# Windowed attention, forward and backward, on one core: gradient loads held behind a transpose, a fourth y/z buffer, and whole 128x128 products in place of split ones

## The chip, the cores and the metric

The kernel runs on one core of one Trainium2 chip. The metric is the device time of the whole program in microseconds (us). Each figure is the median of several executions.

In this kernel TensorE multiplies matrices, VectorE (DVE) and ScalarE (ACT) copy its results out of its output memory, PSUM (they "evict" them), and do the softmax, POOL issues one queue of DMAs (gradient loads and output stores) and the sync engine (SP) issues the other (x loads and all DMA transposes). In the timelines below each engine works through its own instructions in the order in which the program gives them.

## The reference, cut to what matters

```python
# x, grad_out: (1, 256, 256, 384) bf16; windows of 8 x 8 = 64 tokens, C = 384 channels
qkv = xw @ wqkv                       # per window: 64 x 384
p = softmax(q @ k.T * C ** -0.5)
out = (p @ v) @ wo
# returned: out, and the gradients of x, wqkv and wo for grad_out
```

There are 1024 windows. The kernel takes eight at a time, a "quad" of four tiles of 128 tokens, so there are 128 steps. The weights are multiplied together once, at the start; the weight gradients are accumulated over the steps.

## The kernel before

The work on one quad is spread over four steps: loading and projecting (`a`), scores and softmax (`b`), the rest of the attention (`c`), and the gradient of x (`dx`, `d`). The names in what follows: `xq` and `dq` are x and the gradient of the output as loaded; `xT` and `dT` are their transposes, which `project` multiplies into `yz`; `tok` is the transpose of `yz`; `Uq` is a product of the attention and `UT` its transpose, which `dx` needs; `osb` and `dsb` are the buffers from which the output and the gradient of x are stored. `filler` is a piece of the weight gradients. What the change and the argument touch:

```python
def load(st):                                    # issued LEAD = 3 steps ahead
    st["xq"] = xq = grp.tile([P, QUAD, C], BF16, tag="xq", bufs=2 * GQ + 4)
    st["dq"] = dq = qp.tile([P, QUAD, C], BF16, tag="dq", bufs=6)
    for t in range(QUAD):
        nc.sync.dma_start(out=xq[:, t, :], in_=dram_tile(x, bp, t0 + t))
        nc.gpsimd.dma_start(out=dq[:, t, :], in_=dram_tile(grad_out, bp, t0 + t))

def to_channels(st, src, name):                  # dT <- dq, xT <- xq, UT <- Uq
    st[name] = dst = qp.tile([P, QUAD, CK, P], BF16, tag=name, bufs=3 if name == "xT" else 2)
    nc.sync.dma_start_transpose(out=..., in_=st[src]...)

def product(out, lhsT, rhs, start, stop):        # split: two column tiles of 128x64
    if split[0]:
        for h in (LO, HI):
            nc.tensor.matmul(out[h], lhsT=lhsT[:, h], rhs=rhs, start=start, stop=stop)
    else:
        nc.tensor.matmul(out, lhsT=lhsT, rhs=rhs, start=start, stop=stop)

# ... project: y/z evicted by ScalarE into st["yz"], bufs=3
# ... to_tokens: tok <- yz, a DMA transpose on nc.sync

def step(d, c, b, a):                            # the order of one step; cut
    B(scores) ... B(values) ... A(project) ... filler(1)
    pw = C_(attend, (2, 3)) ; B(turn)
    C_(to_channels, "Uq", "UT")
    C_(attend_end, (2, 3), pw)
    split[0] = True
    D_(dx, (0, 1)) ; filler(1)                   # needs tok and UT of the quad
    split[0] = False
    pw = B(attend, (0, 1)) ; B(attend_end, (0, 1), pw) ; D_(dx, (2, 3))

for i in range(-1, n + 2):
    to_channels(get(i + 2), "dq", "dT")
    to_channels(get(i + 2), "xq", "xT")
    load(get(i + LEAD))
    to_tokens(c)
    step(d, c, b, a)
```

So in every step the sync engine issues, in this order, `dT`, `xT`, four x loads, `tok`, `UT`. POOL issues four gradient loads and then the stores, each when its tile has been evicted.

## Time and profile before

| | before |
|---|---|
| time, median of 3 (lowest to highest) | 2145.0 us (2144.54 to 2149.26) |
| TensorE busy | 95% of the span |
| DMA engines busy, in every slice but the last | 90% or more |
| one step, mean over the span (score product to score product) | 16.3 us |
| one step in which TensorE never stalls | 14.8 us |

The two step times in the last rows are read from the timeline. The busy shares alone name two candidates for the bound. The Trainium skill ("Trainium Kernel Development and Optimization", "Performance Expectations") warns that matmul busy time is a bad metric for how close a kernel is to its roofline (the best that the chip allows), because matmuls are pipelined; this trace agrees: TensorE is "95% busy" although an average step is 1.5 us longer than it needs.

These lines are of the page of the kernel before: an engine with its busy time, share and instructions; the DMA engines' busy share in 40 slices; and the two DMA queues with packets, MB and the time of their packets as a share of 16 engines. q1 is the sync engine's queue, q0 POOL's.

```profile
PE 2021.4 (95%) x19046; PEld 1183.3 (55%) x19046; DVE 1280.2 (60%) x2851; ACT 1455.3 (68%) x3213; POOL 1122.7 (53%) x2054
...
DMA  9999999999999999999999999999999999999995
...
q1 hardware_dynamic: 1074384, 304.15, 85.6%
q0 software_dynamic: 98304, 151.39, 27.5%
```

Which of the two paces the step is told by who waits for whom. From the waits of the kernel before (engine and line, what it waited for; total us, times, longest us):

```profile
ACT yz L138 <- DMA tok<-yz: 328.0, 99, 7.2
...
PE po L242 <- ACT yz L138: 45.5, 72, 3.9
```

ScalarE is about to evict y/z and finds its buffer still being read by the `tok` transpose of an older quad. TensorE then waits for ScalarE. In the timeline (start us, length us, what, and in brackets the idle time before it) one such place looks like this:

```profile
1029.05 1.07 ACT L138 CAST yz<-pj 128x512 bf16<-128x512 f32 x2 [3.85 <-DMA tok<-yz]
...
1031.49 0.35 PE L242 MATMUL po<-uq,PS 64*64 64x384 bf16 x2 [0.85 <-ACT yz L138]
```

The transpose is late because the queue that issues it is. The sync engine's timeline shows no pause between its instructions, only about 0.1 to 0.2 us:

```profile
1008.25 1.47 SPq L116 DMA_TRANSPOSE UT<-Uq  x1
1009.94 3.12 SPq L116 DMA_TRANSPOSE dT<-dq  x1
1013.24 1.69 SPq L116 DMA_TRANSPOSE xT<-xq  x1
1014.98 2.89 SPq L111 DMA_DIRECT2D xq<-in_x_dram  x4
1017.98 6.78 SPq L144 DMA_TRANSPOSE tok<-yz  x1
1024.85 2.88 SPq L116 DMA_TRANSPOSE UT<-Uq  x1
1027.95 1.80 SPq L116 DMA_TRANSPOSE dT<-dq  x1
```

And that engine waits for hardly anything but the DMAs before its own.

```profile
SPq L116 <- DMA dq<-in_grad_out_dram: 1.3, 2, 0.9
```

(The larger entries of that view name compute instructions that were over long before; what they show is the time that the queue took to accept the transfer.) So the sync engine's queue, mostly transposes, paces the kernel: by this trace `UT` is issued 7.8 us (median) after its input is complete, and `dT` 9.0 us after its gradient has landed. The POOL queue, which has time to spare, issues its gradient loads right after the stores of the step, at 1011.57, 1.7 us before `xT` is issued:

```profile
1010.48 1.07 POOL L233 DMA_DIRECT2D out_dram<-dsb  x2 [2.44 <-DMA out_dram<-osb]
1011.57 2.11 POOL L112 DMA_DIRECT2D dq<-in_grad_out_dram  x4
1016.54 2.27 POOL L231 DMA_DIRECT2D out_dram<-osb  x4 [2.85 <-ACT osb L249]
```

The cost of splitting products is read from the chain of work that ended last (start us, length us, what and how many): 12 half products of `dx` against 6 whole ones, and 24 against 12 of the weight gradient.

```profile
2095.11 0.97 PE pd L124 x12
2096.08 1.95 PE pg L124 x24
...
2099.09 1.08 PE pd L126 x6
2100.17 1.95 PE pg L126 x12
```

### The profile page before, as it was taken

The numbers are of one execution on the slowest core, as the hardware profiler recorded it, in microseconds if no ns is written. First come the engines' busy times: TensorE is split into PE (matmuls) and PEld (weight loads), VectorE is DVE, ScalarE is ACT, GpSimd is POOL, SyncE is SP. The second block draws the span as 40 slices with busy tenths as digits, with TensorE's granted clock in tenths as the row PEclk, the third lists the DMA queues.
The fourth block names the chain that finished last, engine by engine and source line by source line (L and its number), as shares of the span: only waits on it lengthen the run. The fifth ranks groups of instructions, "written<-read, shape, count | busy, mean of one in ns | idle before, by whom it ended". The sixth has DMA issues, their size and how long they took to land. (4 is left out here: it accounts for less than half of the span.)

```text
span 2135.8 us, 51378 instructions
## 1 busy us (share of the span) xinstructions
PE 2021.4 (95%) x19046; PEld 1183.3 (55%) x19046; DVE 1280.2 (60%) x2851; ACT 1455.3 (68%) x3213; POOL 1122.7 (53%) x2054
## 2 busy tenths in 40 slices
PE   8899999999999999999999999999999999999998
PEld 4555555555555555555555555555555555555555
DVE  6565565656565656656565665665656565665664
ACT  6667676766676667767676766766666676666673
POOL 4554555555555545545454555554555455555543
PEclk9999999999999999999999999999999999999999
DMA  9999999999999999999999999999999999999995
GB/s 210 220 225 220 217 219 211 224 221 219 215 219 213 225 206 225 218 212 222 215 218 213 216 224 211 218 220 218 216 212 221 211 220 222 222 223 211 220 208 123
DMA packets 1173339, 459.11 MB, mean 215 GB/s; under 512 B 1056864, under 2 KB 1147744, under 8 KB 1173088
## 3 DMA queue, kind: packets, MB, share of 16 engines
q1 hardware_dynamic: 1074384, 304.15, 85.6%
q0 software_dynamic: 98304, 151.39, 27.5%
q8 instruction: 149, 2.44, 0.5%
q14 instruction: 102, 0.84, 0.1%
q10 hardware_dynamic: 400, 0.29, 0.0%
HBM read 101.84 MB, written 101.84 MB: 95 GB/s over the span
## 5 line engine op out<-in xcount | busy, mean ns | idle before, releaser
L231 POOL DMA_DIRECT2D out_dram<-osb x1024 | 578.3, 571 | 682.9 <-ACT osb L249 637.3
L138 ACT CAST yz<-pj 128x512 bf16<-128x512 f32 x384 | 213.4, 588 | 360.6 <-DMA tok<-yz 328.0
L286 DVE TENSOR_TENSOR GF_acc<-pg,GF_acc 128x384 f32<-128x384 f32 x258 | 143.9, 558 | 471.8 <-PE pg L124 269.0
L249 ACT CAST osb<-po 128x384 bf16<-128x384 f32 x512 | 225.1, 501 | 211.3 <-issue 174.8
L112 POOL DMA_DIRECT2D dq<-in_grad_out_dram x512 | 270.6, 537 | 174.2 <-DMA out_dram<-osb 63.8
L233 POOL DMA_DIRECT2D out_dram<-dsb x512 | 275.4, 541 | 136.4 <-DMA out_dram<-dsb 62.4
L250 DVE CAST Uq<-pu 128x384 bf16<-128x384 f32 x512 | 264.7, 550 | 54.9 <-PE pu L242 53.0
L126 PE MATMUL pv<-B_sb,xT 128*128 128x384 bf16 x1536 | 270.6, 326 | 0.0
L126 PE MATMUL pj<-xT,A_sb 128*128 128x512 bf16 x1152 | 269.5, 379 | 0.9 <-DMA xT<-xq 0.9
L126 PE MATMUL pj<-dT,BT_sb 128*128 128x512 bf16 x1152 | 269.5, 379 | 0.0
L224 ACT CAST uq<-pv 128x384 bf16<-128x384 f32 x512 | 242.7, 475 | 35.5 <-PE pv L126 33.3
L261 ACT CAST Wq<-pw 64x384 bf16<-64x384 f32 x512 | 242.5, 474 | 9.2
L273 ACT CAST dsb<-pd 128x384 bf16<-128x384 f32 x512 | 222.0, 482 | 26.0 <-ACT Wq L261 7.5
L124 PEld LDWEIGHTS <-xq 128*64 128x64 bf16 x3024 | 204.6, 111 | 45.6
L126 PEld LDWEIGHTS <-xq 128*128 128x128 bf16 x1560 | 152.6, 98 | 114.0
L140 ACT CAST yz<-pj 128x512 bf16<-128x512 f32 x384 | 201.3, 603 | 1.2 <-PE pj L126 1.1
L126 PEld LDWEIGHTS <-A_sb 128*128 128x128 bf16 x1152 | 112.6, 98 | 137.1 <-DMA xT<-xq 1.4
L242 PE MATMUL po<-uq,PS 64*64 64x384 bf16 x1024 | 145.0, 338 | 45.9 <-ACT yz L138 45.5
L126 PEld LDWEIGHTS <-xT 128*128 128x128 bf16 x1536 | 141.5, 98 | 82.8
L124 PE MATMUL pg<-Wq,xq 128*64 128x384 bf16 x2016 | 182.0, 329 | 0.0
L166 DVE TENSOR_REDUCE mx<-sd 64x4 f32<-64x256 f32 x256 | 108.1, 422 | 122.6 <-PE sd L153 118.6
L126 PE MATMUL pg<-Uq,xq 128*128 128x384 bf16 x1032 | 181.6, 326 | 0.0
(66 smaller groups left out, 2674.9 us busy)
## 6 DMA issues: line engine op xcount, KB each, us to landing
xq<-in_x_dram SPq DMA_DIRECT2D x512, 96.0 KB, 3.7
dq<-in_grad_out_dram POOLq DMA_DIRECT2D x512, 96.0 KB, 4.8
out_dram<-osb POOLq DMA_DIRECT2D x1024, 48.0 KB, 5.3
out_dram<-dsb POOLq DMA_DIRECT2D x512, 96.0 KB, 5.5
dT<-dq SPq DMA_TRANSPOSE x128, 6.5
xT<-xq SPq DMA_TRANSPOSE x128, 5.1
tok<-yz SPq DMA_TRANSPOSE x128, 10.2
UT<-Uq SPq DMA_TRANSPOSE x128, 6.4
```

The lines of the kernel that those rows point to most:

```text
L112: nc.gpsimd.dma_start(out=dq[:, t, :], in_=dram_tile(grad_out, bp, t0 + t))
L124: nc.tensor.matmul(out[h], lhsT=lhsT[:, h], rhs=rhs, start=start, stop=stop)
L126: nc.tensor.matmul(out, lhsT=lhsT, rhs=rhs, start=start, stop=stop)
L138: nc.scalar.copy(out=yz[:, mo, :, 0:4:3, :], in_=pj[:])
L140: nc.scalar.copy(out=yz[:, mo, :, 1:3, :], in_=pj[:])
L224: nc.scalar.copy(out=st["uq"][:, t, :], in_=pj[:])
L231: nc.gpsimd.dma_start(out=to[WIN * w:WIN * (w + 1)], in_=src[h, :])
L233: nc.gpsimd.dma_start(out=to, in_=src[:])
L249: nc.scalar.copy(out=osb[:], in_=po[:])
L250: nc.vector.tensor_copy(out=st["Uq"][:, t, :], in_=pu[:])
L261: nc.scalar.copy(out=st["Wq"][h, pair[1], :], in_=pw[1][o, :])
L273: nc.scalar.copy(out=dsb[:], in_=pd[:])
```

## The change

The intent is to move the gradient loads from beside the transposes `UT`/`dT`/`xT` to beside the x loads (a one-element POOL copy from `xT` into the gradient tile makes the loads wait until `xT` has landed), to take away ScalarE's wait for a y/z buffer, and to issue fewer TensorE instructions.

```diff
-    def load(st):
+    def load(st, behind=None):
         ...
+        if behind is not None:
+            nc.gpsimd.tensor_copy(out=dq[0:1, 0, 0:1], in_=behind["xT"][0:1, 0, 0, 0:1])
         for t in range(QUAD):
             nc.sync.dma_start(out=xq[:, t, :], in_=dram_tile(x, bp, t0 + t))
             nc.gpsimd.dma_start(out=dq[:, t, :], in_=dram_tile(grad_out, bp, t0 + t))
     ...
     def product(out, lhsT, rhs, start, stop):
-        if split[0]:
-            for h in (LO, HI):
-                nc.tensor.matmul(out[h], lhsT=lhsT[:, h], rhs=rhs, start=start, stop=stop)
-        else:
-            nc.tensor.matmul(out, lhsT=lhsT, rhs=rhs, start=start, stop=stop)
+        nc.tensor.matmul(out, lhsT=lhsT, rhs=rhs, start=start, stop=stop)
     ...
-            st["yz"] = qp.tile([P, CK, QUAD, 4, WT], BF16, tag="yz", name="yz", bufs=3)
+            st["yz"] = qp.tile([P, CK, QUAD, 4, WT], BF16, tag="yz", name="yz", bufs=4)
     ...
-                load(get(i + LEAD))
+                load(get(i + LEAD), get(i + 2))
```

More of the change, by code (lines that the diff above doesn't have):

```diff
@@ L117, in to_channels @@
                                     in_=st[src][:].rearrange("p t c -> p (t c)"))
-    split = [False]
     def product(out, lhsT, rhs, start, stop):
-        if split[0]:
-            for h in (LO, HI):
-                nc.tensor.matmul(out[h], lhsT=lhsT[:, h], rhs=rhs, start=start, stop=stop)
-        else:
-            nc.tensor.matmul(out, lhsT=lhsT, rhs=rhs, start=start, stop=stop)
+        nc.tensor.matmul(out, lhsT=lhsT, rhs=rhs, start=start, stop=stop)
     def project(st, kind, mo):
         if kind == 0 and mo == 0:
-            st["yz"] = qp.tile([P, CK, QUAD, 4, WT], BF16, tag="yz", name="yz", bufs=3)
+            st["yz"] = qp.tile([P, CK, QUAD, 4, WT], BF16, tag="yz", name="yz", bufs=4)
         yz = st["yz"]
@@ L325, in step @@
         C_(attend_end, (2, 3), pw)
-        split[0] = True
         D_(dx, (0, 1))
         filler(1)
-        split[0] = False
         pw = B(attend, (0, 1))
```

## The prediction

> **What bounds the kernel now.** By the page, TensorE is busy 95% of the span and the 16 DMA engines 90% or more in every slice, so either may be the bound; the timeline tells which. One of the 128 steps (score product to score product) takes 14.8 us when TensorE never stalls, 16.4 us on average. In a slow step ScalarE waits 3 to 4 us at its first y/z eviction for the DMA transpose of an older y/z buffer (the waits: 328.0 us, 99 times), and the attention products stretch behind it. But that transpose is late because the sync engine's DMA queue is. In the timeline that queue issues without a pause: 5.4 us for `tok`, about 2.5 for `UT`, 2.9 for `dT`, 2.2 for `xT`, 2.6 for four x loads, small gaps: about 16.4 us, the whole step. It issues each 3 to 10 us after the compute it needs is done, so it waits for DMA alone. The transposes set the pace; the y/z wait is where TensorE feels it.
>
> **What each part does.**
>
> 1. *Four y/z buffers* put a step (16 us) more between a buffer's uses. The 328 us wait should nearly vanish. But TensorE then runs ahead only until `dx` needs `UT`[...]. The stall moves there; my estimate for this part alone is 0 to 10 us.
>
> 2. *Held gradient loads.* Now they issue about 8.6 us after `tok`, beside `UT`/`dT`. Held until `xT` lands (5.1 us after issue), they issue 6 to 8 us later, beside the x loads and the start of `tok`. The Trainium skill ("DMA: Bandwidth & Descriptors", "Issuing engines are not separate DMA queues") says all queues share the same 16 engines and interleave; the trace agrees: transposes move about 197 GB/s without POOL traffic and about 94 beside 150 to 200 GB/s of it, about 0.5 byte lost per byte. Beside x loads the loss is about half of that. Were all 393 KB of a step moved there, a step would gain about 0.8 us; the overlap is partial and output stores are pushed into `tok`, so I estimate 0.3 to 0.4 us net, 40 to 50 us in all. Against it, a new loop: `xT` landing, four POOL issues (0.54 us each), landing (5 us), `dT` issue, `xT` issue and landing, about 15.7 us by medians; the gradient has only about 1 us to spare before `dT`.
>
> 3. *No split.* 24 half-width products take 1.95 us, 12 full ones 1.95 us. The switch from 128x64 to 128x128 tiles now comes inside `dx(0,1)`: 12 split products took 0.97 us, 6 whole ones 1.08, so about 0.1 us a step, 14 us if exposed, mostly hidden. The skill ("TensorEngine Tiling (Array Packing)", "Key Properties") says a change of tiling mode drains the array; 0.1 us fits.
>
> **Sum.** 2145 less about 45 (held loads), less 5 (buffers), plus about 5 (split), rounded: 2095 us, range 2035 to 2150. Faster by over 2%: 0.54; within 2%: 0.38; slower: 0.08.
>
> **What would show it.** ScalarE's wait for `tok` gone; new waits of `pd` for `UT`; the sync queue still without pauses but with a shorter period; gradient issue just after `xT` lands; transposes faster beside `UT`/`dT`; TensorE's unstalled step about 14.9 us.
>
> **What would make it wrong.** If the y/z stall itself limits the rate, the gain is larger, down to about 1980 us. If gradients land too late for `dT`, the sync queue pauses and the step grows. If stores held behind the loads keep output buffers, ScalarE waits for them.

## The result, and the profile after

The changed kernel takes 2241.88 us (median of 3; 2226.64 to 2246.63), against 2145.0 us. The ratio is 1.043 (95% interval 1.035 to 1.051): slower by 4.3%. Ratios here and below are the mean time of one kernel's runs over that of the other's runs of the same rounds, so they are not quite the ratio of the medians quoted. Executions over 1.5% slower than the fastest of the same kernel are left out of the means. All runs were correct unless said otherwise.

The same lines of the page, after. Nothing there tells the reason: the same work is spread over more time, and the DMA engines still read 90% or more in all slices but the last.

```profile
PE 2013.3 (90%) x16766; PEld 1076.4 (48%) x16766; DVE 1264.1 (57%) x2851; ACT 1467.9 (66%) x3213; POOL 1145.3 (51%) x2180
...
DMA  9999999999999999999999999999999999999996
...
q1 hardware_dynamic: 1074384, 304.15, 80.9%
q0 software_dynamic: 98304, 151.39, 27.7%
```

The waits after. The wait of ScalarE for `tok` at its y/z eviction is gone from the list, and TensorE waits for `UT` instead, both as predicted (and for `tok`, 71.3 us). New are a ScalarE wait for output buffers (until earlier stores have landed), POOL's wait in the new copy, and, by the list, POOL's waits in front of a store until gradient loads have landed:

```profile
ACT osb L245 <- DMA out_dram<-osb: 369.6, 215, 5.3
POOL dq L111 <- DMA xT<-xq: 363.7, 77, 12.8
...
POOL out_dram L229 <- DMA dq<-in_grad_out_dram: 175.0, 89, 6.1
...
PEld L122 <- DMA UT<-Uq: 79.7, 103, 2.5
...
PE pd L122 <- DMA UT<-Uq: 49.7, 76, 2.2
```

And the sync engine, which waited 1.3 us in all for gradients, now waits 217.2 us:

```profile
SPq L118 <- DMA dq<-in_grad_out_dram: 217.2, 237, 5.1
```

Its timeline has the pause in it. `UT` ends at 1017.81, `dT` starts at 1019.91:

```profile
1011.66 4.32 SPq L140 DMA_TRANSPOSE tok<-yz  x1
1016.08 1.73 SPq L118 DMA_TRANSPOSE UT<-Uq  x1
1019.91 1.43 SPq L118 DMA_TRANSPOSE dT<-dq  x1
1021.51 3.04 SPq L118 DMA_TRANSPOSE xT<-xq  x1
1024.61 3.19 SPq L113 DMA_DIRECT2D xq<-in_x_dram  x4
1027.92 4.06 SPq L140 DMA_TRANSPOSE tok<-yz  x1
```

POOL's side of the same step: the copy that waits for `xT`, then the four gradient loads, then the stores; and the next copy one step later.

```profile
1013.30 0.18 POOL L111 COPY dq<-xT 1x1 bf16<-1x1 bf16 x1 [6.58 <-PE pv L122]
1013.87 2.11 POOL L114 DMA_DIRECT2D dq<-in_grad_out_dram  x4 [0.39 <-POOL dq L111]
1015.95 2.28 POOL L227 DMA_DIRECT2D out_dram<-osb  x4
...
1029.55 0.18 POOL L111 COPY dq<-xT 1x1 bf16<-1x1 bf16 x1 [6.12 <-DMA xT<-xq]
```

Read together, these two timelines close a circle. The copy at 1013.30 ends the wait for `xT`; 0.57 us later the gradient loads start, and POOL has issued them 2.11 us after that, at 1015.98. `dT` needs all four of them and is issued 3.93 us later, at 1019.91. `xT` comes behind `dT` on the same queue, 1.60 us later. Its landing lets the next copy go 8.04 us later, at 1029.55. The sum is 16.25 us, and there is no slack in it anywhere: each piece starts when the one before it ends. (The row at 1013.30 puts its wait down to a TensorE product, but `xT` had landed only 0.15 us before.) Over the whole trace, `dT` is issued within 0.3 us of the landing of its last gradient load, and the copy starts within 0.5 us of the landing of `xT`, in 123 of 125 steps: the circle is closed almost always. Averaged over these steps, the five pieces come to 17.0 us (the 17.1 us in the expectations leave out the first and last steps). The score products are 17.0 us apart over the whole span (before: 16.3).

### The profile page after: what moved, and what is told of

The parts are those of the page before. It is cut to its first block, busy times and chain, and to the rows that moved or that the text cites. A ratio compares the mean times of both kernels' runs of the same rounds, so it can differ in the third digit from the quotient of the medians.

```text
span 2224.9 us, 47198 instructions
## 1 busy us (share of the span) xinstructions
PE 2013.3 (90%) x16766; PEld 1076.4 (48%) x16766; DVE 1264.1 (57%) x2851; ACT 1467.9 (66%) x3213; POOL 1145.3 (51%) x2180
## 5 line engine op out<-in xcount | busy, mean ns | idle before, releaser
L245 ACT CAST osb<-po 128x384 bf16<-128x384 f32 x512 | 236.5, 480 | 622.8 <-DMA out_dram<-osb 369.6
L122 PEld LDWEIGHTS <-xq 128*128 128x128 bf16 x3072 | 310.3, 101 | 231.6 <-issue 30.8
L122 PE MATMUL pd<-AT_sb,UT 128*128 128x384 bf16 x1536 | 314.2, 344 | 51.0 <-DMA UT<-Uq 49.7
L111 POOL COPY dq<-xT 1x1 bf16<-1x1 bf16 x126 | 22.4, 178 | 613.2 <-DMA xT<-xq 363.7
L122 PE MATMUL pg<-Wq,xq 128*128 128x384 bf16 x1536 | 285.3, 338 | 0.0
L122 PE MATMUL pg<-Uq,xq 128*128 128x384 bf16 x1536 | 279.5, 333 | 0.0
L263 PE MATMUL pd<-tok,ps 128*64 128x384 bf16 x1024 | 146.9, 340 | 140.7 <-DMA tok<-yz 71.3
L220 ACT CAST uq<-pv 128x384 bf16<-128x384 f32 x512 | 234.4, 482 | 18.7 <-PE pv L122 17.0
L122 PEld LDWEIGHTS <-UT 128*128 128x128 bf16 x1536 | 133.8, 101 | 189.0 <-DMA UT<-Uq 79.7
L134 ACT CAST yz<-pj 128x512 bf16<-128x512 f32 x384 | 220.9, 589 | 4.0 <-PE pj L122 0.2
L136 ACT CAST yz<-pj 128x512 bf16<-128x512 f32 x384 | 201.3, 603 | 0.2
```

Of the source, the lines that this page charges most:

```text
L134: nc.scalar.copy(out=yz[:, mo, :, 0:4:3, :], in_=pj[:])
L136: nc.scalar.copy(out=yz[:, mo, :, 1:3, :], in_=pj[:])
L220: nc.scalar.copy(out=st["uq"][:, t, :], in_=pj[:])
L245: nc.scalar.copy(out=osb[:], in_=po[:])
L263: nc.tensor.matmul(pd[o, :], lhsT=st["ps"][:, w, t, :], rhs=st["tok"][:, :, t, w, :], start=True, stop=False)
```

## The experiments

The theories that were set against each other:

- **LOOP**: the hold makes the circle above, `xT` of one quad, gradient of the next, `dT`, `xT` of the next. It lasts a whole step and sets its length.
- **STORES**: POOL works in order, so the hold also delays the stores behind the loads. Output buffers come free late, ScalarE waits (369.6 us) and stalls TensorE.
- **ARRAY**: the whole products, or TensorE running further ahead, cost the time.

### Without the hold, and the hold alone

The changed kernel with one line undone:

```diff
-                load(get(i + LEAD), get(i + 2))
+                load(get(i + LEAD))
```

> The changed kernel without the hold (four y/z buffers and whole products stay). Theories: LOOP = the hold closes a circle through the gradient (xT landing, copy, four POOL issues, landing, dT, xT, landing) that now takes a whole step of 17.1 us; STORES = output stores stand behind the held loads in POOL's order, output buffers come free late, ScalarE waits for them (369.6 us) and stalls TensorE; ARRAY = the whole products or the further lead of TensorE cost the time. LOOP and STORES: 2120 to 2155 us, the sync queue's waits for the gradient (217 us) under 20. ARRAY: stays at 2200 or more.

Measured: 2142.61 us (before in the same rounds: 2153.68), ratio 0.996 (0.992 to 1.000). The sync engine's wait for gradients is gone:

```profile
SPq L118 <- DMA dq<-in_grad_out_dram: 1.8, 3, 0.9
```

The kernel before with the hold and nothing else of the change:

> The kernel before with the hold alone (three y/z buffers, split products). LOOP and STORES: as slow as the whole change, 2200 to 2260 us, with the sync queue waiting for gradient landings some 200 us. ARRAY: 2145 within 1%.

Measured: 2274.5 us, ratio 1.056 (1.050 to 1.062), even slower than the whole change, a little over what was expected. The sync engine waits again:

```profile
SPq L118 <- DMA dq<-in_grad_out_dram: 260.6, 236, 3.9
```

The hold is the whole loss. The rest of the change alone gives about 0.4%, at the edge of what these rounds can tell from nothing, and ARRAY has fallen. With only three y/z buffers the hold costs more than with four: by its trace the circle is closed in 122 of 125 steps and is 17.5 us long. ScalarE's wait for `tok` is back there and has grown to 464.9 us.

### Circle or stores: two runs that take away one and keep the other

All loads one step earlier, with one more buffer for each; the hold, and what stands behind it on POOL, as it was. Now a gradient load held behind `xT` is needed a whole step later.

```diff
-    LEAD = 3
+    LEAD = 4
-        ... tag="xq", name="xq", bufs=2 * GQ + 4)
-        ... tag="dq", name="dq", bufs=6)
+        ... tag="xq", name="xq", bufs=2 * GQ + 5)
+        ... tag="dq", name="dq", bufs=7)
```

> The changed kernel with all loads one step earlier (lead 4, one more x and one more gradient buffer); the hold stays where it is, so POOL's order and the delay of the stores are unchanged, but the circle through the gradient now spans two steps. LOOP: the sync queue's wait for gradients falls under 20 us and the time to 2090 to 2150. STORES: ScalarE still waits 300 us or more for output buffers and the time stays over 2200.

Measured: 2127.93 us, ratio 0.990 (0.985 to 0.994). Of the sync engine's wait for gradients little is left,

```profile
SPq L118 <- DMA dq<-in_grad_out_dram: 1.4, 1, 1.4
```

while ScalarE still waits for output buffers most of what it did (241.5 of 369.6 us), which then costs nothing that shows:

```profile
ACT osb L245 <- DMA out_dram<-osb: 241.5, 169, 5.2
```

The mirror image: the hold and the lead of 3 stay, and the output buffers are doubled.

```diff
-            osb = ob.tile([P, C], BF16, tag="o", name="osb")
-            dsb = ob.tile([P, C], BF16, tag="d", name="dsb")
+            osb = ob.tile([P, C], BF16, tag="o", name="osb", bufs=8)
+            dsb = ob.tile([P, C], BF16, tag="d", name="dsb", bufs=8)
```

> The changed kernel with eight output buffers of each kind in place of four; the hold stays. LOOP: ScalarE's wait for output buffers (369.6 us) goes, but the time stays within 1.5% of 2240 (2205 to 2275) and the sync queue still waits about 217 us for gradients. STORES: back to 2120 to 2160.

Measured: 2240.68 us, ratio 1.042 (1.038 to 1.047), as slow as the change. ScalarE's wait for the `osb` buffers has fallen from 369.6 us to 5.5 us; the sync engine's wait stands:

```profile
SPq L118 <- DMA dq<-in_grad_out_dram: 220.0, 231, 4.1
```

LOOP got both runs right, STORES both wrong.

### Circles of other lengths

If the circle's length is what counts, shorter circles must cost less. Two were tried. In the first, the copy reads `dT` of the same quad, which lands about 3 us before `xT`:

```diff
-            nc.gpsimd.tensor_copy(out=dq[0:1, 0, 0:1], in_=behind["xT"][0:1, 0, 0, 0:1])
+            nc.gpsimd.tensor_copy(out=dq[0:1, 0, 0:1], in_=behind["dT"][0:1, 0, 0, 0:1])
```

> The changed kernel with the same copy, but it reads dT, which lands about 3.0 us before xT (means of the changed kernel's trace). LOOP: the circle then has 14 us of latency, less than the DMA queue's own 16.4 us step; the sync queue's wait for gradients falls from 217 us to under 40 and the time to 2125 to 2170 us. If any hold at all costs the time: over 2200.

Measured: 2163.61 us, ratio 1.004 (0.998 to 1.009), and

```profile
SPq L118 <- DMA dq<-in_grad_out_dram: 38.3, 43, 2.5
```

In the second the copy stands between the second and the third load, so the last two are held and only two issues lie on the circle:

```diff
         for t in range(QUAD):
+            if behind is not None and t == 2:
+                nc.gpsimd.tensor_copy(out=dq[0:1, 2, 0:1], in_=behind["xT"][0:1, 0, 0, 0:1])
```

> The changed kernel with the copy moved between the second and third gradient load: two loads of four are held, and the circle is shorter by two POOL issues (1.07 us): about 16.0 us, close to the DMA queue's own step. LOOP: a time between, 2140 to 2205 us, with 50 to 150 us of the sync queue's waits for gradients. If it is not the length of the circle: as the whole hold, 2225 to 2260.

Measured: 2160.34 us, ratio 1.005 (1.000 to 1.011), and

```profile
SPq L118 <- DMA dq<-in_grad_out_dram: 110.9, 160, 2.6
```

Last, the copy alone, without its wait (it reads the identity matrix in place of `xT`):

```diff
-            nc.gpsimd.tensor_copy(out=dq[0:1, 0, 0:1], in_=behind["xT"][0:1, 0, 0, 0:1])
+            nc.gpsimd.tensor_copy(out=dq[0:1, 0, 0:1], in_=ident[0:1, 0:1])
```

> The changed kernel with the copy kept, but reading a constant, so that it waits for no transpose. Copy's own cost (0.18 us on POOL, 126 times) is off the critical path: 2120 to 2155 us, as without the hold. If the copy or its semaphores cost the time: over 2200.

Measured: 2129.03 us, ratio 0.991 (0.986 to 0.995). The copy itself is free. Waits of the sync engine for gradients of 2.5, 38, 111 and 217 us go with ratios of 0.991, 1.004, 1.005 and 1.043. The order is the expected one, but it is not a straight line: the first 100 us of waits cost little, the next 100 much. The traces tell why. With the copy behind `dT` the circle is closed in only 33 of 125 steps. With half the loads held it is closed in 105 of 125, but it is only 16.5 us long there, hardly more than the 16.3 us step of the kernel without the hold. What counts is by how much the circle is longer than the step that the kernel would have without it, and not the sum of the waits in it.

### The two other parts of the change, alone

Four y/z buffers in the kernel before (`bufs=3` to `bufs=4`):

> The kernel before with four y/z buffers alone. If the DMA queue of the sync engine sets the pace (as predicted): ScalarE's 328 us wait for tok vanishes, the stall moves to TensorE's wait for UT, and the time changes by 0 to -10 us (ratio 0.995 to 1.0). If the y/z wait itself sets the pace: 2000 to 2080 us.

Measured, over five rounds: 2152.5 us (before: 2158.15), ratio 0.998 (0.995 to 1.002). ScalarE's 328 us wait is gone and the wait has moved to TensorE's loads of `UT`, as predicted:

```profile
PEld L124 <- DMA UT<-Uq: 130.3, 106, 3.2
```

Whole products in the kernel before (`split[0] = True` to `False`):

> The kernel before with whole products alone. If TensorE's extra change of array mode (about 0.1 us a step) is hidden behind the DMA queue: ratio 0.998 to 1.004. If it is exposed: about +14 us, ratio 1.006 to 1.008. ARRAY (the whole products cost the time): 1.02 or more.

Measured: 2150.84 us, ratio 0.997 (0.994 to 1.000). No cost, perhaps a small gain.

### What the place of the gradient loads is worth

With the lead of 4 the circle doesn't bind, so the predicted gain of the hold can be looked for. The same kernel without the hold:

> The changed kernel with loads one step earlier (lead 4) and without the hold: against the run with lead 4 and the hold (ratio 0.990) it tells what the hold's better place for the gradient loads is worth once its circle no longer binds. If the place beside the x loads is worth what I predicted (0.3 to 0.4 us a step): this run is 1.5 to 2.5% slower than that one, so ratio 1.005 to 1.015. If the place is worth nothing: ratio within 0.5% of 0.990.

Measured: 2142.34 us (before: 2158.15), ratio 0.994 (0.991 to 0.997), against 0.990 (0.985 to 0.994) with the hold, from other rounds. The intervals overlap, and the run with the copy that waits for nothing also had 0.991. The gain is 0.4% by these means, about 9 us; with these intervals it can be anything from nothing to about 0.9%, and it is not shown to be there at all.

The same with the hold and eight buffers for the attention output:

> Lead 4 with the hold and eight buffers for the attention output. ScalarE's wait for output buffers (241.5 us with lead 4) goes. If the DMA queue sets the pace, the time stays within 0.5% of ratio 0.990; if the delayed stores still cost time there, it falls to 0.975 to 0.985 and is the best kernel so far.

Measured: 2135.99 us, ratio 0.991 (0.988 to 0.993), as without the buffers, and 0.3% under the last run, which is of the same rounds. With them ScalarE's wait moved to the other output's buffers (153.3 us) and cost nothing, so the late stores cost nothing here either.

### What paces the kernel before

My predicted gain rested on the shared DMA engines: a byte less beside the transposes was to give them half a byte. That can be tested by taking POOL's traffic away. The second output is stored in the last band only (a wrong result):

```diff
-            store(out_1, st, t, dsb, False)
+            if st["at"][0] == NBP - 1:
+                store(out_1, st, t, dsb, False)
```

> The kernel before without the stores of the second output except in its last band (wrong result on purpose): 393 KB of 3.5 MB less DMA traffic a step, all of it off any engine's wait but the DMA engines' time. If the DMA engines set the pace, as predicted: about 0.5 byte of transposes gained per byte, 1.2 us a step, 1970 to 2040 us, sync queue still without pauses or TensorE at its 14.8 us step. If the compute engines or fixed DMA latencies set it: 2145 within 1%.

Measured: 2097.79 us (before: 2151.0), ratio 0.975 (0.971 to 0.980). Neither expectation holds. The 393 KB a step are worth about 53 us, 0.4 us a step, a third of what I had worked out from the transposes' rates. So more runs were made. First, as many bytes out of the sync engine's own queue: the transpose `UT` is left out and `dx` multiplies a constant (again wrong).

```diff
-        C_(to_channels, "Uq", "UT")
-                product(pd[:], st["UT"][:, t, m, :], AT_sb[:, m, :], False, m == CK - 1)
+                product(pd[:], B_sb[:, t % CK, m * P:(m + 1) * P], AT_sb[:, m, :], False, m == CK - 1)
```

> The kernel before without the UT transpose (dx reads a constant of the same shape; wrong result on purpose): 393 KB a step less, out of the sync engine's queue. SERIAL (that queue's own chain of transfers sets the pace): about 2.5 us a step less, down to TensorE's unstalled step: 1930 to 1990 us. SHARED (bytes on the 16 engines set the pace, whatever queue): as little as the stores, ratio 0.96 to 0.98, 2065 to 2110 us.

Measured: 1946.09 us, ratio 0.904 (0.901 to 0.907). TensorE is now the bound, with steps of 14.8 us. The granted clock is higher, 0.999 against 0.974 to 0.985 in the runs of the kernel before, but that is not the gain: a step of the kernel before without a stall takes 14.8 us too.

```profile
PE 1923.1 (99%) x19046; PEld 1104.9 (57%) x19046; DVE 1263.6 (65%) x2851; ACT 1464.2 (75%) x3213; POOL 1123.1 (58%) x2054
```

The same number of bytes is thus worth almost four times as much in a transpose as in stores, and TensorE's own step hides whatever more there may have been. Then the x loads, as many bytes again, were moved from that queue to POOL's, first in the changed kernel without the hold, then with a lead of 4 and eight output buffers as well:

```diff
-            nc.sync.dma_start(out=xq[:, t, :], in_=dram_tile(x, bp, t0 + t))
+            nc.gpsimd.dma_start(out=xq[:, t, :], in_=dram_tile(x, bp, t0 + t))
```

> The changed kernel without the hold, x loads issued by POOL in place of the sync engine; the same traffic in all. SERIAL: the sync queue loses 2.6 us a step and the time falls to 1980 to 2070 us, unless the stores, 2 us later in POOL's order, keep output buffers. SHARED: 2120 to 2155 us, as without the hold.

> As the last, with lead 4 and eight attention output buffers, so that later loads and stores wait for nothing. SERIAL: 1970 to 2050 us, the fastest of all. SHARED: ratio 0.985 to 0.995.

Measured: 2387.6 us, ratio 1.110 (1.106 to 1.114), and 2230.15 us, ratio 1.038 (1.034 to 1.042; median and ratio are of the three fast runs, 2228 to 2242; three more were slow). Both expectations missed, in the wrong direction, but neither run is a clean test of a shorter list. In the first, POOL's longer list of loads delays the gradient again (the sync engine waits 371.5 us for it). In the second that wait is small (30.5 us), but the longest wait of the list is now ScalarE's for a buffer of the gradient of x, which still had four of them, until POOL's earlier stores had landed:

```profile
ACT dsb L269 <- DMA out_dram<-dsb: 503.0, 256, 7.8
```

The sync engine has become one that waits for compute: `UT` is issued 0.03 us (median) after its input is complete, against 7.8 us in the kernel before. The longest transpose became slower as well: `tok` takes the queue 6.6 us by the median, where before it took 5.4 us, and up to 11.1 us; two long ones:

```profile
999.90 9.40 SPq L140 DMA_TRANSPOSE tok<-yz  x1
...
1017.13 10.45 SPq L140 DMA_TRANSPOSE tok<-yz  x1
```

So these two runs do not tell what a shorter list on that queue is worth. What is shown is that one transpose less on it is worth far more than as many bytes less of stores (0.904 against 0.975), and that my rate did not foresee what traffic beside the transposes costs. Whether the x loads in that queue cost as much as a transpose, and how the DMA engines divide themselves between the two queues, stays open.

### A version that beats both

If the transposes pace the kernel, one of them should be done elsewhere. In the changed kernel without the hold, `UT` is made by TensorE, just before `attend(0, 1)`:

```diff
-        C_(to_channels, "Uq", "UT")
+    def turn_U(st):
+        st["UT"] = dst = qp.tile([P, QUAD, CK, P], BF16, tag="UT", name="UT", bufs=2)
+        for t0 in (0, 2):
+            pt = ring.tile([P, 2, CK, P], BF16, tag="r", name="pU")
+            for i in range(2):
+                for m in range(CK):
+                    nc.tensor.transpose(pt[:, i, m, :], st["Uq"][:, t0 + i, m * P:(m + 1) * P], ident[:])
+            nc.vector.tensor_copy(out=dst[:, t0:t0 + 2, :, :], in_=pt[:])
+        C_(turn_U)
```

> The changed kernel without the hold, with the UT transpose moved from the DMA to TensorE (12 transposes of 128x128 a step, two evictions by VectorE), correct result. If the DMA transposes set the pace: TensorE's step of 14.9 us plus about 0.8 us of transposes, 15.6 us, so 1990 to 2080 us, faster than both kernels. If not: 2130 us or more.

Measured: 2061.59 us (before: 2150.16), ratio 0.959 (0.957 to 0.962), correct. It beats the kernel before by 4.1% and the changed one by far more; against the same kernel with `UT` by DMA (0.996, other rounds) the move is worth about 3.7%. Its steps are 15.7 us long, and TensorE is busy nearly throughout:

```profile
PE 2041.9 (99%) x18302; PEld 1161.6 (56%) x18302; DVE 1382.0 (67%) x3107; ACT 1464.9 (71%) x3213; POOL 1121.7 (54%) x2054
```

The work added to a step is small, by the timeline:

```profile
1010.96 0.83 PE L130 MATMUL pU<-ident,Uq 128*128 128x128 bf16 x12
...
1011.63 1.01 DVE L131 COPY UT<-pU 128x768 bf16<-128x768 bf16 x2
```

And with the hold put back:

> The same with the hold. LOOP: the circle is a latency of its own, 16 to 17 us a step, hardly shorter without UT, so the hold costs even more against its twin without it: 2090 to 2230 us, at least 3% above it, with 150 us or more of the sync queue's waits for gradients. If the hold only cost time because the DMA engines were full: within 1.5% of its twin.

Measured: 2204.02 us, ratio 1.026 (1.023 to 1.029), so 6.9% above its twin without the hold. The sync engine has fewer transposes to issue and simply waits longer:

```profile
SPq L118 <- DMA dq<-in_grad_out_dram: 528.8, 240, 6.2
```

The circle is therefore a bound of its own. With a fifth of the transposed bytes taken away (185 GB/s moved in place of 206) it is still closed in 123 of 125 steps and holds the step near 17 us. It is not a matter of the granted clock either, which was 0.994 in this profile and 0.977 in that of the changed kernel.

## Why the prediction was wrong, point by point

**The direction** was wrong: 2095 us was predicted, with 0.08 for slower by over 2%, and 2241.88 us was measured.

**The step that failed** is the one on the held loads: "Against it, a new loop: ... about 15.7 us by medians; the gradient has only about 1 us to spare before `dT`." The loop was found and named, as the prediction's second way of being wrong, and then treated as a remark, because 15.7 is less than 16.4. Measured, the loop lasts 17.0 us, longer than the step. The medians came from the kernel before, where these transfers had other neighbours. Two terms were too small. The last gradient load of a quad now lands 6.1 us after its issue in place of 4.9 (medians of the two traces). And the start of the loads after the landing of `xT`, copy included, takes 0.7 us that I had left out. From the issue of `dT` to the landing of `xT` nothing changed in sum (8.4 us; 8.5 before): `xT` lands later after its issue, 6.5 in place of 5.1 us, but is issued sooner after `dT`, 2.0 in place of 3.0 us. Giving the loop a second step (lead of 4) takes the loss away (0.990), as removing the hold does, and shortening the loop takes most of it away; doubling the output buffers takes away nothing.

**The gain of the held loads**, 40 to 50 us, is not there. Its place in the trace was right (the loads did move), its value was not: about 9 us by the means with the loop out of the way, and perhaps nothing. The term that was mis-sized is "about 0.5 byte lost per byte", worked out from how fast transposes moved in moments with more or less POOL traffic. It was a correlation. So was the guess that beside x loads only half of it is lost: counted over all bytes of the sync engine's queue in 1 us stretches of the trace, it is 0.6 byte per byte there against 0.7 beside transposes (POOL at about 120 GB/s), which leaves little to gain. Taking 393 KB a step away from POOL bought 0.4 us where this figure said 1.2 us.

**Four y/z buffers**: right. 0 to 10 us were predicted, 0.2% (about 4 us) was measured, with an interval that includes nothing; the wait moved to `UT` as said.

**No split**: "0.1 us a step, mostly hidden" was right in that it costs nothing; the measured 0.3% goes the other way. The 0.1 us is there in TensorE's own step without a stall, 14.94 us with whole products against 14.83.

**What bounds the kernel before**: right in its core, that the transposes pace the step and that the y/z wait is only where it is felt (0.904 without one transpose, 0.998 without the y/z wait). Unproven in the rest: that every transfer of the queue counts alike. The runs that took the x loads out of it had new waits of their own (371.5 and 503.0 us) and do not tell.

**Signs**: the `tok` wait gone, yes; `pd` waiting for `UT`, yes; loads right after `xT`, yes; TensorE's unstalled step of 14.9 us, yes (the shortest steps in the steady part of the changed kernel's trace are 14.9 us). Transposes faster beside `UT`/`dT`, half: `dT` takes the queue 1.6 us in place of 2.9, but `UT` 2.5 as before, and `xT` 3.0 in place of 2.2 (medians). "The sync queue still without pauses but with a shorter period": no, and this was the sign that decided.

## What to carry to other kernels

Before holding one transfer behind another, follow the new dependency around until it meets itself, add up its latencies under the load they will then have, and treat a sum within some 10% of the step as binding (here it came out 8% longer than predicted, 17.0 us for 15.7); giving the held transfer one more step of lead is the cure, if the buffers are there. A hold on an in-order queue buys a better place only at the price of everything that now comes later, so measure first what the better place is worth, by taking that traffic away. When DMA transposes pace a kernel and TensorE has slack, moving one of them to TensorE can be worth more than rearranging the loads: here it was worth 3.7%, and no rearrangement of the loads was worth more than about 1%.

## What the Trainium skill lacked or had wrong

- "DMA: Bandwidth & Descriptors", "Rules for kernel authors", says that spreading DMAs over issuing engines for bandwidth does not help, since all run on the same 16 engines. Here it did worse than not help: moving the x loads from the sync engine to POOL cost 11.0%, and 3.8% with more lead and buffers. The page does not warn that the longer list delays what stands behind it in that engine's order (371.5 us of waits for gradients in one run, 503.0 us for output buffers in the other), and it has no figure for a transpose beside other traffic (`tok`: 6.6 us in the queue in place of 5.4 us).
- The same page's "Alternative transpose paths" lists TensorE as another way to transpose, and does not say there when the move pays. Moving one of four transposes (393 KB a step) to TensorE and VectorE gave about 3.7%; leaving it out altogether gave 9.6%.
- "TensorE: Matmul & The Clock Gate", "Part 4: PE-mode transpose", gives about 275 ns for a 128x128 bf16 transpose in one kernel's context. Here one took 219 ns by the profile, but 12 of them 0.83 us together, so about 70 ns each in sequence. TensorE's step without a stall grew by 0.87 us for the 12 (14.94 to 15.81 us), so the second number is the one to plan with.
- "TensorEngine Tiling (Array Packing)", "Key Properties", says that a change of tiling mode drains the array, without a cost. Here 6 whole products behind the change took 1.08 us where 12 half ones without it took 0.97 us, and the whole kernel was not slower for it (0.997), since TensorE's step was not its bound.
- No page says that a wait put into an in-order queue can close a circle through another queue; here such a circle of 17.0 us cost 4.3%.
